# Infini-attention with a GLU: the memory recalls of a segment as sixteen products on the array's quarters, from a dense memory

## The chip, the cores and the metric

The kernel runs on one core of a Trainium2 chip. The metric is device time in microseconds (us), as the median of several runs; smaller is better. A core has TensorE (PE in the profile; its weight loads are PEld), VectorE (DVE), ScalarE (ACT), GpSimd (POOL) and SyncE (SP), which work side by side and wait for one another through semaphores. SP and POOL also issue DMAs; a queue issues in order, so a DMA that waits for its data holds up those behind it. TensorE's results go to PSUM, eight banks of 128 partitions x 512 f32.

## The reference

Two branches read the same normalised input, and both are added to x:

```python
xn = _layernorm(x, axis=-1)
return x + _A_ref(xn, A_wq, A_wk, A_wv, A_wo, A_beta) + _B_ref(xn, B_w_gate, B_w_up, B_w_down)
```

x has 2048 rows of 448. `_B_ref` is a gated FFN, `(sigmoid(xn Wg) * (xn Wu)) Wd`, of inner width 1792. `_A_ref` splits the rows into 4 segments of L = 512 and the columns into 16 heads of 28:

```python
for s in range(N):
    qs, ks, vs = q[:, :, s], k[:, :, s], v[:, :, s]
    logits = jnp.einsum("bhqd,bhkd->bhqk", qs, ks) * scale + mask
    p = _softmax(logits, axis=-1)
    a_dot = jnp.einsum("bhqk,bhkd->bhqd", p, vs)
    pq = phi(qs)
    num = jnp.einsum("bhld,bhde->bhle", pq, M)
    den = jnp.einsum("bhld,bhd->bhl", pq, z)[..., None] + 1e-6
    a_mem = num / den
    o = g * a_mem + (1.0 - g) * a_dot
    outs.append(o)
    pk = phi(ks)
    M = M + jnp.einsum("bhld,bhle->bhde", pk, vs)
    z = z + jnp.einsum("bhld->bhd", pk)
```

Here phi(t) is t + 1 above zero and exp(t) elsewhere; it is an infini-attention with a memory M (28 x 28 per head) and its normaliser z. `a_mem` is called a recall below. Segment 0 has none, since its memory is empty.

## The kernel before

Most products are made of f32 halves: each f32 operand is split into a high and a low part (type fp32r), and `TERMS` lists the 11 products of parts that make one exact product over the 448 columns. A block is a segment of 512 tokens, b = 0 to 3, in four pieces t of 128.

The program has two phases. In the first, the pool `front`, the order of PE, ACT and DVE is the order of the source; SP and POOL are ordered by the scheduler. In the second, PE and SP keep the source's order: three generators are interleaved there, `ffn` (the gated FFN), `attention()` (scores, softmax, and the products with the values, L672) and `project()`. The `ffn` starts in the last block of `front` already, a step for each `next(ffn)`.

In `front`, each block goes through these steps.

- `values(b, t)` (L334): the values of 128 tokens, 11 products into the bank pair `p`; ACT stores them as `vst`, each head in 32 columns: 28 values, then ones. The ones make z a column of the memory.
- `keys_queries(b, c)` (L339), c = 0 to 6: 128 rows of keys and queries, transposed, 448 of each. ACT and DVE split them into `qk`, and SP writes them to `qd` in DRAM (L352). ACT and DVE also make phi of them in `e`; the queries' phi (c from 3) goes to `fd` in DRAM by an SP DMA (L357).
- `key_rows` (L359): TensorE transposes phi of the keys into `kn`, tokens on partitions.
- `update(b, i)` (L369), i = 0 to 3 for a group of four heads: keys by values, four matmuls into a 112 x 128 bank; a mask `heads` keeps the blocks on the diagonal, and the result is added to `mst[n][i]`. A group's memory is thus a block diagonal, 112 rows (4 heads of 28) by 128 columns (4 heads of 32), mostly zeros, in two copies that change places with each block.
- `phi_queries(b, i)` (L381): an SP DMA brings group i's 112 rows of `fd` back to SBUF, from partition 0 on. It shares the five buffers tagged `e`.
- `recall(b, i, phi)` (L386): one f32 matmul, 112 x 128 by 512 tokens, into bank `m` or `pd`. The trace shows an f32 matmul as two passes. DVE then turns it (`ts`, L391: transposes of 32 x 32 blocks), weighs it by the gate and by 1 / z (`weigh`, L127 to L131), and turns it back (`tb`, L393); one POOL DMA writes it to `od` in DRAM (L394), to which attention's part is added later.

Block b has the four recalls of segment b-1, for b = 2 and 3: one after each of values 1, 2 and 3, and one after the first keys. The recalls of segment 3, the last, stand in the last block: after its sixth and seventh `keys_queries` (k = 5 and 6), and then after two steps each (`FILLS`) of the `ffn`. Each recall has a bank, a `ts` (one buffer) and a `tb` (two).

Further names: `ready_down` splits a down weight (`wdn`, ACT and DVE, L85 and L86) that `load_down` brought by SP (`rawd` or `raw`, L185); `begin` holds three such steps that run in the last block. `ready_up` does this for `wgu`. In the FFN, a pair of banks holds the gate and the up product (L240); ACT takes the tanh of the gate into `sg` (L248), DVE multiplies (L249), and ACT and DVE split the result into `hh` (L251, L252). `sg` is one of two buffers of `two_k` (512 f32 per partition). The banks are `p` 2, `s` 2, `m` 1, `gu` 2 and `pd` 1; the gate products take `gu`, the up products `p`, the scores `s` (L597, copied out by ACT, L601).

`G.tensor_copy` in `normalise` lets POOL copy the tail of a normalised piece that `turn` (L95) transposes for the next block.

Of the kernel before, what the change touches and what calls it, by code (L numbers as in the profile page):

```python
# [16 lines left out]
P = 128  # L17
D = 448
# [39 lines left out]
WARM = 10  # L58


@with_exitstack
def kernel(
# [56 lines left out]
    gate = keep.tile([P, NG], F32, name="gate")  # L119
# [148 lines left out]
    with tc.tile_pool(name="front", bufs=2) as sb, tc.manual_schedule(engines=FRONT):  # L268
        heads = sb.tile([P, P], F32, name="heads", bufs=1)
# [5 lines left out]
        mst = [[sb.tile([GW, P], F32, name=f"mst{n}_{i}", bufs=1) for i in range(NG)] for n in range(2)]  # L275
# [63 lines left out]
        def keys_queries(b, c):  # L339

            qk = four_k(F32R, "qk")
            pp = bank("pp", ("p", "gu" if b < NB - 1 else "s")[c % 2])
            for n, (a, w) in enumerate(TERMS):
                T.matmul(pp, wqk[c][:, w, :], xs[b][:, a, :], start=n == 0, stop=n == len(TERMS) - 1)  # L344
            A.activation(qk[:, 0, :], pp, AF.Copy)
            e = None
            if (c < 4 and b < NB - 1) or (c > 2 and b > 0):
                e = sb.tile([P, L], F32, name="e", tag="e", bufs=5)
                A.activation(e, pp, AF.Relu, scale=-1.0)  # L349
                A.activation(e, e, AF.Exp, scale=-1.0)  # L350
            V.tensor_sub(qk[:, 1, :], pp, qk[:, 0, :].bitcast(F32))  # L351
            nc.sync.dma_start(qd[b][c * P:(c + 1) * P], qk.bitcast(F32))  # L352
            if e is not None:
                V.scalar_tensor_tensor(e, pp, 0.0, e, op0=ALU.max, op1=ALU.add)
                if c > 2 and b > 0:
                    lo = max(c * P - D, 0)
                    nc.sync.dma_start(fd[b][lo:(c + 1) * P - D], e[D + lo - c * P:])  # L357
            return e

        def key_rows(c, e):  # L360

            pk = bank("pk", ("m", "pd")[c % 2])
            for t in range(NT):
                T.transpose(pk[:, t * P:(t + 1) * P], e[:, t * P:(t + 1) * P], ident)  # L364
            n = min(P, D - c * P)
            A.activation(kn[:, :, c * P:c * P + n], pk.rearrange("p (t n) -> p t n", t=NT)[:, :, :n], AF.Copy)

        def update(b, i):

            pmm = bank("pmm", ("pd", "m")[i % 2])  # L370
            for t in range(NT):
                T.matmul(pmm[:GW, :P], kn[:, t, i * GW:(i + 1) * GW], vst[:, t, HG * i:HG * (i + 1), :],  # L372
                         start=t == 0, stop=t == NT - 1)
            if b == 0:
                V.tensor_mul(mst[1][i], pmm[:GW, :P], heads[:GW])
            else:
                dm = sb.tile([GW, P], F32, name="dm")
                V.tensor_mul(dm, pmm[:GW, :P], heads[:GW])
                V.tensor_add(mst[(b + 1) % 2][i], mst[b % 2][i], dm)

        def phi_queries(b, i):  # L381
            phi = sb.tile([GW, L], F32, name="phi", tag="e", bufs=5)
            nc.sync.dma_start(phi, fd[b][i * GW:(i + 1) * GW])
            return phi

        def recall(b, i, phi):  # L386
            ts = sb.tile([P, L], F32, name="ts", bufs=1)
            tb = sb.tile([P, L], F32, name="tb", bufs=2)
            n2 = bank("n2", ("m", "pd")[i % 2])
            T.matmul(n2, mst[b % 2][i], phi, start=True, stop=True)  # L390
            V.transpose(ts, n2)  # L391
            weigh(sb, ts, gate[:, i:i + 1], MEM_EPS)
            V.transpose(tb, ts)  # L393
            nc.gpsimd.dma_start(od[b][P * i:P * (i + 1)], tb)  # L394
# [18 lines left out]
        with nc.allow_non_contiguous_dma(reason="a strip's heads"):  # L413
            for j in range(HG):
                nc.sync.dma_start(gate[32 * j:32 * j + 32], beta[j::HG].partition_broadcast(32))
# [50 lines left out]
        for t in range(2):  # L466
# [18 lines left out]
        G.memset(heads, 1.0)  # L485
        h3 = heads.rearrange("p (j c) -> p j c", c=32)
        G.affine_select(h3, h3, pattern=[[-DH, HG], [0, 32]], base=0, channel_multiplier=1,
                        compare_op=ALU.is_ge, fill=0.0)
        G.affine_select(h3, h3, pattern=[[DH, HG], [0, 32]], base=DH - 1, channel_multiplier=-1,
                        compare_op=ALU.is_ge, fill=0.0)  # L490

        ffn = gated()
        for b in range(NB):
            last = b == NB - 1
            phi, xn = {}, {}
            if b > 1:
                phi = {i: phi_queries(b - 1, i) for i in range(NG)}
            st = None
            for t in range(3 if b == 0 else 0, NT):
                values(b, t)  # L500
                if b > 1 and t > 0:
                    recall(b - 1, t - 1, phi[t - 1])
# [15 lines left out]
            for k, c in enumerate((3, 4, 5, 6, 0, 1, 2) if last else range(7)):  # L518
# [3 lines left out]
                if k == 0:  # L522
                    if b > 1:
                        recall(b - 1, NG - 1, phi[NG - 1])
# [4 lines left out]
                    if b == 0:  # L529
# [3 lines left out]
                        V.tensor_scalar(gate_n, gate, -1.0, 1.0, op0=ALU.mult, op1=ALU.add)  # L533
                if last:
                    if k > 0:
                        next(ffn)
                    if 2 <= k < 6:
                        phi[k - 2] = phi_queries(b, k - 2)
                    if k > 4:
                        begin[k - 5]()  # L540
                        recall(b, k - 5, phi[k - 5])
# [14 lines left out]
            if last:  # L556
                for i in range(2):
# [4 lines left out]
                    recall(b, i + 2, phi[i + 2])  # L562
# [256 lines left out]
```

## Time and profile before

| | |
|---|---|
| median of 3 runs | 697.25 us (696.43 to 699.18) |
| span of the profiled execution | 697.6 us |
| TensorE | 690.0 us busy, 99% of the span, 3594 instructions |
| VectorE | 570.2 us, 82% |
| ScalarE | 343.6 us, 49% |
| GpSimd | 148.5 us, 21% |
| DMA packets | 45797, 84.37 MB, mean 121 GB/s |
| DMA issues of recalls: `phi<-fd`, `od<-tb` | 12 each, of 224 and 256 KB |

The profile is of one execution. A timeline row begins with the start in us from the span's start and the time to its last end; "x11" is a run of eleven instructions shown as one row, and its length contains the fill of the array, so that successive rows overlap. In a table of stretches, each engine's busy time and number of instructions follow the bounds and the length (PE, DVE, ACT, POOL, SP), then come the granted TensorE clock, the DMA engines' busy share and GB/s. A row of grouped instructions has the count, the busy sum and the mean of one in ns, then the idle time ahead of them and what ended it. "<-" names what was waited for. The chain of waits follows the end back to what released each step, so its shares say which work sets the time.

### The profile page before, as it was taken

To read this page: it belongs to the slowest core of one execution; us is meant where nothing else is said; L and a number is where in the kernel's file an instruction comes from. 1 tells how busy PE (TensorE), PEld (TensorE's weight loads), DVE (VectorE), ACT (ScalarE), POOL (GpSimd) and SP (SyncE) were. 2 spreads that over 40 slices of the span, in tenths; PEclk is the share of its full clock that TensorE was granted. 3 is DMA by queue.
4 is the path that set the end of the run, shared out by engine and by line. 5 is a ranking of instruction groups with operands and counts; after the bars stand their busy time and mean duration, and the time that the engine had idled before them with its cause. 6 is when DMAs were issued, how large, how long until landed. Compare 5 with 4: busy or idle time off the path is not lost.

```text
span 697.6 us, 10438 instructions
## 1 busy us (share of the span) xinstructions
PE 690.0 (99%) x3594; PEld 567.7 (81%) x3594; DVE 570.2 (82%) x994; ACT 343.6 (49%) x563; POOL 148.5 (21%) x349
## 2 busy tenths in 40 slices
PE   8989999999999999999999999999999999999997
PEld 7878878777878787877878778787787878778897
DVE  6665687658789898988898889998898889889863
ACT  5646646344455455543655446455644555446320
POOL 4400010101222131322222222132221322222000
PEclk9999999999999999999999999999999999999999
DMA  7833545687222423234323343324242432333342
GB/s 265 320 130 149 201 185 211 226 300 224 70 77 65 120 86 85 48 113 108 78 58 96 70 128 66 98 56 114 74 108 66 95 70 60 86 94 88 91 152 105
DMA packets 45797, 84.37 MB, mean 121 GB/s; under 512 B 6321, under 2 KB 20401, under 8 KB 45233
## 3 DMA queue, kind: packets, MB, share of 16 engines
q1 hardware_dynamic: 42736, 76.37, 35.3%
q0 software_dynamic: 3008, 7.34, 5.2%
q8 instruction: 28, 0.46, 0.3%
q14 instruction: 25, 0.20, 0.1%
HBM read 51.05 MB, written 32.64 MB: 120 GB/s over the span
## 4 chain that ended last, share of the span: by engine, by line
PE 94%; DMA 2%; DVE 1%; ACT 1%; SPq 0%; issue 0%; ACTq 0%
PE pgu L240 42%; PE pd L166 20%; PE pp L344 9%; PE st L597 5%; PE pa L672 5%; PE po L756 5%; PE pv L326 4%; PE pmm L372 2%; PE n L390 1%; DMA qd<-qk 1%; DMA acc<-in_x 1%; PE pt L95 1%; PE pk L364 1%; DVE stats L285 0%; ACT L512 0%
## 5 line engine op out<-in xcount | busy, mean ns | idle before, releaser
L240 PE MATMUL pgu<-xs,wgu 128*128 128x512 f32 x1232 | 321.0, 398 | 0.0
L240 PEld LDWEIGHTS pgu<-xs,wgu 128*128 128x128 f32 x1232 | 226.6, 188 | 48.0 <-issue 3.2
L166 PE MATMUL pd<-wdn,hh 128*128 128x448 f32 x672 | 162.4, 368 | 0.0
L612 POOL TENSOR_SCALAR_AFFINE_SELECT w<-w 128x256 f32<-128x256 f32 (+1 forms) x160 | 81.7, 512 | 254.1 <-ACT w L601 215.1
L166 PEld LDWEIGHTS pd<-wdn,hh 128*128 128x128 f32 x672 | 123.2, 188 | 15.1 <-issue 1.0
L652 ACT ACTIVATE w<-w 128x1024 f32<-128x1024 f32 (+1 forms) x96 | 87.1, 915 | 87.6 <-DVE w L651 87.0
L651 DVE TENSOR_TENSOR w<-w,mb 128x1024 f32<-128x1024 f32 (+1 forms) x96 | 99.7, 1049 | 0.2
L601 ACT ACTIVATE w<-st 128x512 f32<-128x512 f32 x128 | 75.0, 588 | 43.6 <-PE st L597 43.5
L614 DVE TRANSPOSE_TENSOR_REDUCE mx<-w 128x32 f32<-128x1024 f32 x64 | 79.1, 1235 | 12.7 <-POOL w L612 12.7
L344 PE MATMUL pp<-xs,wqk 128*128 128x512 f32 x308 | 80.6, 412 | 0.0
L344 PEld LDWEIGHTS pp<-xs,wqk 128*128 128x128 f32 x308 | 58.1, 192 | 14.8 <-issue 2.4
L169 DVE TENSOR_TENSOR acc<-pd,acc 128x448 f32<-128x448 f32 x112 | 67.4, 602 | 2.7 <-PE pd L166 2.5
L597 PE MATMUL st<-qk 84*128 84x128 f32 (+3 forms) x256 | 64.0, 311 | 0.0
L251 ACT ACTIVATE hh<-sg 128x512 fp32r<-128x512 f32 x56 | 35.1, 627 | 44.5 <-DVE sg L249 35.0
L597 PEld LDWEIGHTS st<-qk 84*128 84x128 f32 x256 | 48.4, 189 | 8.6 <-ACT w L601 0.2
L248 ACT ACTIVATE sg<-pgu 128x512 f32<-128x512 f32 x56 | 33.3, 594 | 40.1 <-PE pgu L240 40.1
L641 DVE STREAM_TRANSPOSE mb<-top 128x1024 f32<-128x1024 f32 x32 | 39.8, 1242 | 10.3 <-POOL top L638 10.1
L351 DVE TENSOR_TENSOR qk<-pp,qk 128x512 fp32r<-128x512 f32 x28 | 19.3, 688 | 34.6 <-ACT e L349 27.3
L249 DVE SCALAR_TENSOR_TENSOR sg<-sg,pgu 128x512 f32<-128x512 f32 x56 | 37.4, 668 | 4.8 <-PE pgu L240 4.8
L252 DVE SCALAR_TENSOR_TENSOR hh<-sg,hh 128x512 fp32r<-128x512 f32 x56 | 38.6, 690 | 2.7 <-ACT hh L251 2.5
L326 PE MATMUL pv<-wv,xs 128*128 128x448 f32 x176 | 39.7, 377 | 0.3
L672 PE MATMUL pa<-w,vv 128*32 128x128 f32 (+3 forms) x512 | 38.4, 436 | 0.0
(100 smaller groups left out, 639.2 us busy)
## 6 DMA issues: line engine op xcount, KB each, us to landing
qk<-qd SPq DMA_DIRECT2D x192, 112.0 KB
qd<-qk SPq DMA_DIRECT2D x28, 512.0 KB
raw<-in_w_ffn SPq DMA_DIRECT2D x14, 512.0 KB
vd<-vst SPq DMA_DIRECT2D x4, 1024.0 KB
vv<-vd SPq DMA_DIRECT2D x16, 256.0 KB
od<-w POOLq DMA_DIRECT2D x16, 256.0 KB, 4.0
sums<-od SPq DMA_DIRECT2D x32, 128.0 KB
out<-acc SPq DMA_DIRECT2D x16, 224.0 KB
```

What stands on the lines that cost most here:

```text
L166: T.matmul(pd[:, :D], l, r, start=n == 0, stop=n == len(mms) - 1)
L169: V.tensor_add(acc[b][:, t, :], pd[:, :D], acc[b][:, t, :])
L240: T.matmul(dst, wgu[f][:, w, side * P:(side + 1) * P], xs[b][:, a, :], start=n == 0, stop=n == len(TERMS) - 1)
L326: T.matmul(pv[:, :D], xs[b][:, a, t * P:(t + 1) * P], wv[w], start=n == 0, stop=n == len(TERMS) - 1)
L344: T.matmul(pp, wqk[c][:, w, :], xs[b][:, a, :], start=n == 0, stop=n == len(TERMS) - 1)
L597: T.matmul(st[:, at:at + L - kb * P], self.qk[:KS, 1, h, kb * P:(kb + 1) * P], self.qk[:KS, 0, h, kb * P:], start=True, stop=True)
L601: A.activation(w, st, AF.Copy)
L612: G.affine_select(d, d, pattern=pattern, base=0, channel_multiplier=-1, compare_op=ALU.is_ge, fill=MASK)
L614: V.tensor_reduce(mx[:, 16 * (n - 1):16 * (n + 1)], w3[:, n // 2, :2 * L].rearrange("p (b n) -> p b n", n=32), axis=mybir.AxisListType.X, ...
L651: V.tensor_sub(w, w, m)
L652: A.activation(w, w, AF.Exp, scale=SCALE)
L672: T.matmul(pa[32 * j:32 * j + 32, kb * P:], self.vv[:, kb, 32 * j:32 * j + 32], self.pairs[j // 2].block(j % 2, kb), start=kb == 0, stop=k ...
```

## The change

The memory is kept dense. `update(b, j)` multiplies the values of a group of heads (128 columns, as the stationary operand) by its keys: `by_head` reads the keys in four overlapping runs of 32 columns, 28 apart, so that each head's block is 32 x 32. DVE transposes the 128 x 128 result into `dm`, and after the fourth group copies the diagonal blocks of all groups into one 128 x 128 tile, by four copies or additions. Head 4j + i then has its memory at partitions 32i and columns 32j. The columns of `kn` past the last key are set to zero by POOL; the mask `heads` is gone.

`phi_queries` fills one tile, 128 x 4 x 512, by four SP DMAs: DMA i brings the i-th head of all four groups (28 partitions, four rows of 2 KB for each partition) to partitions 32i.

`recall` is one set of sixteen f32 matmuls, each of 28 rows by 32 columns and 512 tokens at its own position of the array, into four banks: row quarter i into bank i. It stands after values 1 of blocks 2 and 3, and in the last block, for segment 3, after the first FILLS of the `ffn`. `recalled(b, i, n2)` does with bank i what the recall's second half did, with `ts` from the buffers of `two_k`, and with four POOL DMAs of 32 partitions (64 KB) in place of one. It stands where the recalls stood in blocks 2 and 3, and after the two FILLS in the last block, two each. A second gate vector has the heads in the new order, filled by four more small DMAs at the start; the buffers tagged `e` are 4, not 5.

```diff
@@ -56,6 +56,7 @@
 FRONT = {mybir.EngineType.PE, mybir.EngineType.Activation, mybir.EngineType.DVE}
 FILLS = (2, 2)
 WARM = 10
+EB = 4
 
 
 @with_exitstack
@@ -116,7 +117,7 @@
         return ps.tile([P, L], F32, name=name, tag=tag, bufs=banks[tag])
 
 
-    gate = keep.tile([P, NG], F32, name="gate")
+    gate = keep.tile([P, NG + HG], F32, name="gate")
     gate_n = keep.tile([P, NG], F32, name="gate_n")
 
     def weigh(pool, num, g, add):
@@ -266,13 +267,12 @@
 
 
     with tc.tile_pool(name="front", bufs=2) as sb, tc.manual_schedule(engines=FRONT):
-        heads = sb.tile([P, P], F32, name="heads", bufs=1)
         stage = eight_k(F32, "stage").rearrange("p (c a) n -> p c (a n)", c=4)
         vst = eight_k(F32, "vst").rearrange("p (t a) (h c) -> p t (a h) c", t=NT, c=32)
         wv = [late_pair("wv") for _ in range(4)]
         wv = [wv[c // 2][:, c % 2, :] for c in range(8)]
         wqk = [sb.tile([P, 8, P], F32R, name=f"wqk{c}", bufs=1) for c in range(7)]
-        mst = [[sb.tile([GW, P], F32, name=f"mst{n}_{i}", bufs=1) for i in range(NG)] for n in range(2)]
+        mst = [sb.tile([P, P], F32, name=f"mst{n}", bufs=1) for n in range(2)]
         one = sb.tile([P, 1], F32, name="one", bufs=1)
         kn = eight_k(F32, "kn").rearrange("p (t a) n -> p t (a n)", t=NT)
 
@@ -345,7 +345,7 @@
             A.activation(qk[:, 0, :], pp, AF.Copy)
             e = None
             if (c < 4 and b < NB - 1) or (c > 2 and b > 0):
-                e = sb.tile([P, L], F32, name="e", tag="e", bufs=5)
+                e = sb.tile([P, L], F32, name="e", tag="e", bufs=EB)
                 A.activation(e, pp, AF.Relu, scale=-1.0)
                 A.activation(e, e, AF.Exp, scale=-1.0)
             V.tensor_sub(qk[:, 1, :], pp, qk[:, 0, :].bitcast(F32))
@@ -357,6 +357,10 @@
                     nc.sync.dma_start(fd[b][lo:(c + 1) * P - D], e[D + lo - c * P:])
             return e
 
+        def by_head(a):
+
+            return bass.AP(a.tensor, a.offset, [list(a.ap[0]), [DH, HG], [1, 32]])
+
         def key_rows(c, e):
 
             pk = bank("pk", ("m", "pd")[c % 2])
@@ -365,33 +369,52 @@
             n = min(P, D - c * P)
             A.activation(kn[:, :, c * P:c * P + n], pk.rearrange("p (t n) -> p t n", t=NT)[:, :, :n], AF.Copy)
 
-        def update(b, i):
-
-            pmm = bank("pmm", ("pd", "m")[i % 2])
+        turned = {}
+
+        def update(b, j):
+
+            if j == 0:
+                turned[b] = two_k("dm").rearrange("p (j n) -> p j n", n=P)
+            dm = turned[b]
+            pmm = bank("pmm", ("pd", "m")[j % 2])
             for t in range(NT):
-                T.matmul(pmm[:GW, :P], kn[:, t, i * GW:(i + 1) * GW], vst[:, t, HG * i:HG * (i + 1), :],
-                         start=t == 0, stop=t == NT - 1)
-            if b == 0:
-                V.tensor_mul(mst[1][i], pmm[:GW, :P], heads[:GW])
-            else:
-                dm = sb.tile([GW, P], F32, name="dm")
-                V.tensor_mul(dm, pmm[:GW, :P], heads[:GW])
-                V.tensor_add(mst[(b + 1) % 2][i], mst[b % 2][i], dm)
-
-        def phi_queries(b, i):
-            phi = sb.tile([GW, L], F32, name="phi", tag="e", bufs=5)
-            nc.sync.dma_start(phi, fd[b][i * GW:(i + 1) * GW])
-            return phi
-
-        def recall(b, i, phi):
-            ts = sb.tile([P, L], F32, name="ts", bufs=1)
+                keys = by_head(kn[:, t, GW * j:GW * j + HG * 32])
+                T.matmul(pmm[:, :P], vst[:, t, HG * j:HG * (j + 1), :], keys, start=t == 0, stop=t == NT - 1)
+            V.transpose(dm[:, j, :], pmm[:, :P])
+            if j == HG - 1:
+                for i in range(NG):
+                    rows = slice(32 * i, 32 * i + 32)
+                    after, before = (mst[(b + n) % 2][rows, :].rearrange("p (j c) -> p j c", c=32) for n in (1, 0))
+                    if b == 0:
+                        V.tensor_copy(after, dm[rows, :, rows])
+                    else:
+                        V.tensor_add(after, before, dm[rows, :, rows])
+
+        def phi_queries(b, phi):
+            for i in range(HG):
+                nc.sync.dma_start(phi[32 * i:32 * i + DH],
+                                  fd[b].rearrange("(j i d) n -> i d j n", i=HG, d=DH)[i])
+
+        def recall(b, phi, tags):
+
+            n2 = [bank("n2", tag) for tag in tags]
+            for i in range(HG):
+                rows = slice(32 * i, 32 * i + DH)
+                for j in range(NG):
+                    cols = slice(32 * j, 32 * j + 32)
+                    T.matmul(n2[i][cols, :], mst[b % 2][rows, cols], phi[rows, j, :], start=True, stop=True,
+                             tile_position=(32 * i, 32 * j))
+            return n2
+
+        def recalled(b, i, n2):
+            ts = two_k("ts")
             tb = sb.tile([P, L], F32, name="tb", bufs=2)
-            n2 = bank("n2", ("m", "pd")[i % 2])
-            T.matmul(n2, mst[b % 2][i], phi, start=True, stop=True)
-            V.transpose(ts, n2)
-            weigh(sb, ts, gate[:, i:i + 1], MEM_EPS)
+            V.transpose(ts, n2[i])
+            weigh(sb, ts, gate[:, NG + i:NG + i + 1], MEM_EPS)
             V.transpose(tb, ts)
-            nc.gpsimd.dma_start(od[b][P * i:P * (i + 1)], tb)
+            for j in range(NG):
+                h = HG * j + i
+                nc.gpsimd.dma_start(od[b][32 * h:32 * h + 32], tb[32 * j:32 * j + 32])
 
         raw = [four_k(F32, "wv_raw") for _ in range(2)]
         raw = [r.rearrange("p a n -> p (a n)")[:, :2 * D] for r in raw]
@@ -412,7 +435,9 @@
         nc.sync.dma_start(raw_qk[6], w_qk[6])
         with nc.allow_non_contiguous_dma(reason="a strip's heads"):
             for j in range(HG):
-                nc.sync.dma_start(gate[32 * j:32 * j + 32], beta[j::HG].partition_broadcast(32))
+                nc.sync.dma_start(gate[32 * j:32 * j + 32, :NG], beta[j::HG].partition_broadcast(32))
+            for j in range(NG):
+                nc.sync.dma_start(gate[32 * j:32 * j + 32, NG:], beta[HG * j:HG * j + HG].partition_broadcast(32))
         G.memset(vst[:, :, :, DH:], 1.0)
         A.activation(gate_n, vst[:, 0, :NG, DH], AF.Sqrt)
 
@@ -482,24 +507,22 @@
         turn_low(3)
         split_qk(1)
         split_qk(2)
-        G.memset(heads, 1.0)
-        h3 = heads.rearrange("p (j c) -> p j c", c=32)
-        G.affine_select(h3, h3, pattern=[[-DH, HG], [0, 32]], base=0, channel_multiplier=1,
-                        compare_op=ALU.is_ge, fill=0.0)
-        G.affine_select(h3, h3, pattern=[[DH, HG], [0, 32]], base=DH - 1, channel_multiplier=-1,
-                        compare_op=ALU.is_ge, fill=0.0)
+        G.memset(kn[:, :, D:], 0.0)
 
         ffn = gated()
         for b in range(NB):
             last = b == NB - 1
-            phi, xn = {}, {}
+            xn = {}
             if b > 1:
-                phi = {i: phi_queries(b - 1, i) for i in range(NG)}
+                phi = sb.tile([P, NG, L], F32, name="phi", bufs=1)
+                phi_queries(b - 1, phi)
             st = None
             for t in range(3 if b == 0 else 0, NT):
                 values(b, t)
+                if b > 1 and t == 1:
+                    n2 = recall(b - 1, phi, ("gu", "gu", "m", "pd"))
                 if b > 1 and t > 0:
-                    recall(b - 1, t - 1, phi[t - 1])
+                    recalled(b - 1, t - 1, n2)
                 if b == 0:
                     split_qk(t)
                 if last:
@@ -521,7 +544,7 @@
                     split_qk(c + 4)
                 if k == 0:
                     if b > 1:
-                        recall(b - 1, NG - 1, phi[NG - 1])
+                        recalled(b - 1, NG - 1, n2)
                     if b == 0:
                         st = rstd(*st)
                     if b < 2:
@@ -530,15 +553,15 @@
                         A.activation(gate, gate, AF.Exp, scale=-1.0)
                         V.tensor_scalar_add(gate, gate, 1.0)
                         V.reciprocal(gate, gate)
-                        V.tensor_scalar(gate_n, gate, -1.0, 1.0, op0=ALU.mult, op1=ALU.add)
+                        V.tensor_scalar(gate_n, gate[:, :NG], -1.0, 1.0, op0=ALU.mult, op1=ALU.add)
                 if last:
                     if k > 0:
                         next(ffn)
-                    if 2 <= k < 6:
-                        phi[k - 2] = phi_queries(b, k - 2)
+                    if k == 3:
+                        phi = sb.tile([P, NG, L], F32, name="phi", bufs=1)
+                        phi_queries(b, phi)
                     if k > 4:
                         begin[k - 5]()
-                        recall(b, k - 5, phi[k - 5])
                     continue
                 if 2 <= k < 6:
                     key_rows(k - 2, e[k - 2])
@@ -559,7 +582,9 @@
                         next(ffn)
                     if i == 0:
                         begin[2]()
-                    recall(b, i + 2, phi[i + 2])
+                        n2 = recall(b, phi, ("s", "s", "m", "pd"))
+                    recalled(b, 2 * i, n2)
+                    recalled(b, 2 * i + 1, n2)
 
 
 
```

## The prediction

> **What bounds the kernel now.** First the page's busy shares and the chain of work that ended last.
>
> ```profile
> PE 690.0 (99%) x3594; PEld 567.7 (81%) x3594; DVE 570.2 (82%) x994; ACT 343.6 (49%) x563; POOL 148.5 (21%) x349
> ...
> PE pgu L240 42%; PE pd L166 20%; PE pp L344 9%; PE st L597 5%; PE pa L672 5%; PE po L756 5%; PE pv L326 4%; PE pmm L372 2%; PE n L390 1%; DMA qd<-qk 1%; DMA acc<-in_x 1%; PE pt L95 1%; PE pk L364 1%; DVE stats L285 0%; ACT L512 0%
> ```
>
> TensorE sets the time, and its order is fixed: a microsecond that it waits is lost, one taken from it is won. The recalls (L390) are 1% of the chain. So I read the TensorE timeline where they stand: segment 1's (three rows), segment 2's first, segment 3's last.
>
> ```profile
> 82.42 4.66 PE L326 MATMUL pv<-wv,xs 128*128 128x448 f32 x22
> 86.92 1.02 PE L390 MATMUL n<-phi,mst 112*128 112x512 f32 x2
> 87.38 2.78 PE L326 MATMUL pv<-wv,xs 128*128 128x448 f32 x11
> 90.00 1.02 PE L390 MATMUL n<-phi,mst 112*128 112x512 f32 x2
> ...
> 124.14 1.02 PE L390 MATMUL n<-phi,mst 112*128 112x512 f32 x2
> ...
> 155.26 0.86 PE L240 MATMUL pgu<-xs,wgu 128*128 128x512 f32 x3
> 155.96 1.02 PE L390 MATMUL n<-phi,mst 112*128 112x512 f32 x2
> ...
> 161.63 7.33 PE L240 MATMUL pgu<-xs,wgu 128*128 128x512 f32 x29
> 168.79 0.40 PE L597 MATMUL st<-qk 84*128 84x512 f32 x1
> ...
> 172.47 0.40 PE L597 MATMUL st<-qk 84*128 84x512 f32 x1
> ```
>
> The shown durations overlap, so costs come from starts. From 86.92 to 90.00 are 3.08 us; 11 value matmuls take half of 4.66 less overlap, 2.21. A recall therefore costs 0.87, two passes of 0.43, and a segment's four 3.47. None of them waits here.
>
> **Part 1, the sixteen products.** Thirty-two passes of 28 rows by 32 columns replace eight. The trace has no product by row quarters; the nearest is the attention product L672, four column quarters with full rows.
>
> ```profile
> 207.72 0.16 PEld L672 LDWEIGHTS pa<-w,vv 128*32 128x32 f32 x8 [0.36 <-POOL w L612]
> 208.18 0.13 PEld L672 LDWEIGHTS pa<-w,vv 128*32 128x32 f32 x4 [0.30 <-issue]
> ```
>
> Weight loads come four at a time, 0.46 us apart: four column quarters share one pass time. Whether row quarters share it too no row shows. Bounds for a segment: 0.87 if all sixteen go together, 4 x 0.87 = 3.47 if only columns do; about 0.3 beside for filling and emptying (also an estimate, from 1.02 against 0.87 twice). I take 1.17: a gain of 2.3 per segment.
>
> The Trainium skill, "TensorEngine Tiling (Array Packing)", Key Properties, lets tiles on different rows and columns run at the same time; by that it is the lower bound, as I took, and the L672 row agrees for columns.
>
> **Part 2, waiting for phi, segments 1 and 2.** Before, copy i needed only its 112 rows, and recalls stood after the second, third and fourth values and the next keys, so that each came 3 us after the one before. Now copy i takes 28 rows from each of the four groups: all four copies need the last feature write (c=6), and all sixteen products stand after the second values.
>
> ```profile
> 83.46 0.32 SPq L357 DMA_DIRECT2D fd<-e  x1
> 86.35 0.79 SPq L383 DMA_DIRECT2D phi<-fd  x2
> ...
> 120.75 0.42 SPq L357 DMA_DIRECT2D fd<-e  x1
> ...
> 124.67 0.79 SPq L383 DMA_DIRECT2D phi<-fd  x2
> ...
> 87.00:87.50 0.50, 0.50 (x4) 0.26 (x2) 0.43 (x3) 0.00 (x0) 0.00 (x0) 1.00 0.40 61
> ...
> 87.25:89.00 1.75, 1.75 (x9) 1.33 (x8) 1.29 (x5) 0.64 (x2) 0.00 (x0) 1.00 0.84 260
> ...
> 206.29 2.47 SPq L580 DMA_DIRECT2D qk<-qd  x6
> 207.25:210.75 3.50, 3.50 (x38) 1.70 (x37) 3.20 (x7) 0.94 (x2) 0.89 (x2) 1.00 0.80 195
> ```
>
> (SP queue; then tables of stretches, last two columns DMA share and GB/s.) The last write is issued at 83.46; the first copies that need it start at 86.35, 2.89 later, and their data rises within about 0.9. So in the changed kernel all four copies start at 86.35, and TensorE is at the recalls at 86.92: it is there before the data. How fast 224 KB land: 112-partition copies ran at 260 GB/s, the 28-partition copies of qk at 195. The new ones have 28 partitions, so I take 195: 1.18 us each (0.86 by 260). First landing near 86.35 + 0.9 + 1.2 + about 0.4 until the semaphore (an estimate) = 88.8, the fourth 3.5 later, 92.3. Rows 0 to 2 run meanwhile; the last row's passes take 0.87 + 0.15, so that values go on at 93.4. Before, TensorE would have had the two values and four recalls behind it, had they stood together, at 86.92 + 3.47 = 90.4. Loss **+3.0**; bounds +1.3 (260 GB/s for all and no time until the semaphore: 86.35 + 0.9 + 3.4 + 1.0 = 91.7) and +4 (1.4 until the semaphore).
>
> Segment 2: TensorE at 124.14, old products done at 127.6; the write issued at 120.75 has landed after the same 2.89 at 123.6, or by the row only at 124.67. The same 7.0 from there to the next values gives +3.0 and +4.1; between them **+3.5**, bounds +1.3 and +4.8. Queued behind the wait on TensorE are the third and fourth values and the keys, so everything that follows.
>
> **Part 3, segment 3.** All sixteen products now stand after the first FFN fill; nothing waits for data there, as the copies are issued four keys earlier. That saves 2.3. But the drain moves to the FFN's start. The order of the changed streams: VectorE must do three recalls before the first multiply of the second gated pair; the recalls' `ts` now shares the two `sg` buffers, so the second and third tanh (L248) wait until `ts` of recalls 2 and 3 are turned into `tb`. And two loads (rawd, raw) now stand on SP behind the write of the last key block.
>
> ```profile
> 87.95:90.68 2.73, 2.29 (x4) 1.00 0.37 127
> ...
> L394 POOL DMA_DIRECT2D od<-tb x12 | 6.7, 559 | 88.2 <-DVE tb L393 85.7 <-DVE tm L304 2.5
> ...
> 152.99 0.35 SPq L185 DMA_DIRECT2D rawd<-in_w_ffn  x1
> 156.81 0.33 SPq L352 DMA_DIRECT2D qd<-qk  x1
> ...
> 158.41 0.56 ACT L85 ACTIVATE wdn<-rawd 128x448 fp32r<-128x448 f32 x1
> 158.68 0.62 DVE L86 TENSOR_TENSOR wdn<-raw,wdn 128x448 fp32r<-128x448 f32 x1
> 160.05 1.22 DVE L86 TENSOR_TENSOR wgu<-raw,wgu 128x1024 fp32r<-128x1024 f32 x1
> 160.44 0.60 ACT L248 ACTIVATE sg<-pgu 128x512 f32<-128x512 f32 x1 [0.52 <-PE pgu L240]
> 163.95 0.67 DVE L249 SCALAR_TENSOR_TENSOR sg<-sg,pgu 128x512 f32<-128x512 f32 x1
> 170.32 0.58 ACT L601 ACTIVATE w<-st 128x512 f32<-128x512 f32 x1
> ```
>
> The first row is one whole recall on VectorE (transpose, weighing, transpose): 2.73. Counted as if nothing before had shifted, the three pgu matmuls start at s = 155.26 - 0.87 = 154.4, since the recall ahead of them (one of two among the last keys) is gone. rawd is issued right behind the write, 156.81 - 0.87 + 0.4 = 156.3; it lands about 3 later (as the 2.89), 159.3; ACT and VectorE split it until 160.5; three recalls and the wgu split, 3 x 2.7 + 1.2 = 9.3, end at 169.8; tanh 0.6: 170.4. TensorE needs that tanh's bank for the fourth pair's gate. A pgu matmul takes 0.23 (29 from 161.63, behind 0.4 of a recall's second pass, to 168.79). Eleven stand ahead of the products, 2.6; products 1.2; then 36 matmuls, 8.4, and a score product, 0.24: it is there at 154.4 + 12.4 = 166.8: stall 3.65. Then VectorE has the fourth `ts`, sg, weighing, hh and `tb`, about 3.6 in all, until 173.8; tanh, sg, hh and the score copy follow with 0.6 each, so the third score product starts at about 176.4, before at 172.47: **+4.0**. Bounds: -2.3 if VectorE keeps up, +5. Were rawd not late, 1.4 less of the stall and +2.5.
>
> **Nothing for the rest.** The update has its four matmuls per group as before and the same number of VectorE operations: ±0.2 by the count. POOL issues 36 more DMAs of 0.56, 20 us of an engine that is 21% busy; its copies for block 3's transposes can stand behind one recall's four, 2.2 us, for which the wait of Part 2 leaves time; with that cover gone, up to +1. Fewer `e` buffers and four small gate loads at the start: covered by loads that SP waits for anyway, ±0.2.
>
> **Sum.** 697.6 + 3.0 + 3.5 + 4.0 = 708.1 against the profiled span; the median of the runs is 0.35 below that span: **708**.
>
> **The rivals.** *The pack without a wait* (faster): the sixteen products start when TensorE gets there. Place: TensorE at 86.92 and 124.14. Point: the fourth copy must land within about 0.9 after that, by 87.8 and 125.0; then 3 x -2.3 = -6.9, 690.4. For it: products do shrink from 3.47 to 1.17. Against: with a write landing at 86.35 the four copies, 0.9 MB, would need over 600 GB/s. *The waits, but no drain problem*: VectorE catches up in segment 3, since its 82% leave room; 697.25 + 3.0 + 3.5 - 2.3 = 701.5. For it: had the loads held nothing up, 9.3 us of work from 157.2, when the first products are out, would end at 166.5, just in time. Against: the loads do stand behind a write, and the shared buffers stay. *Copies land at the 260 rate and complete at once*: Part 2 falls to +1.3 twice: 703.9 with Part 3 at +4.0, 697.6 with Part 3 at -2.3. *The clock*: each wait cools TensorE.
>
> ```profile
> L431 PE MATMUL warm<-ident 128*128 128x128 f32 x20 | 4.6, 430 | 1.5 <-POOL ident masks.py:199 1.5
> ...
> L364 PE MATMUL pk<-ident,e 128*128 128x128 f32 x48 | 7.2, 272 | 0.0
> ```
>
> At the start 20 matmuls took 4.6 us; the same shape later 7.2 x 20 / 48 = 3.0. If each of three waits costs that 1.6 again, 708 + 4.8 = 712.8. The waits are 1 to 4 us long and broken by products of other rows, so perhaps one or none. The Trainium skill, "TensorE: Matmul & The Clock Gate", Part 1, says that some 3.4 us without work halve the clock; by it the stretches here stay mostly just under. *The change does not do what it says*: row quarters follow one another. Then the copies' pitch of 1.18 hides 0.87 per row and the total stays; only if all sixteen go one by one, 13.9 per segment, is it about +35: 733.
>
> **How the numbers follow.** My forecast 60% (its own range 703 to 711), waits without drain problem 17%, fast copies 8%, clock 7%, one by one 3%, pack without a wait 5%. A difference of 0.5%, 3.5 us, is about what a measurement of this kernel can tell from none: 693.8 to 700.7. Faster: the pack without a wait, 0.05. Same: fast copies without drain problem and the lower ends of the waits alone, 0.09. Slower: the rest, 0.86. The range leaves out the pack and one by one, and cuts the clock's tail and the fastest copies: 700 to 712.
>
> **What would show it.** Right: TensorE's idle before the recalls at about 87 and 124, ended by DMA phi, 3 to 5 us in all at each, products of a row under 1.1 us; idle in the FFN's first pairs ended by ACT's tanh, itself waiting on VectorE `tb`; rawd issued after the last qd. Wrong: products starting without a wait; L248 not waiting on L393; rows of the product 3 us apart on a busy TensorE; a granted clock below 1 behind the waits.

## The result, and the profile after

| | median | lowest to highest | ratio to before (95%) |
|---|---|---|---|
| before | 697.16 us | 696.43 to 699.18 | |
| changed | 717.44 us | 715.02 to 719.75 | 1.0283 (1.026 to 1.0307) |

The change costs 20.3 us; 708 with a range of 700 to 712 had been predicted. The direction and the places were right, the size was half.

First the device time and the span. The changed kernel's profiled execution took 716.85 us and its span is 715.1; a second profile of the kernel before (run e4 below) took 697.08 with a span of 695.4. So the time is the span and about 1.7 us, and the first profile of before, with its span of 697.6, came from an execution some 2 us above the median. The stages below are therefore counted against e4's profile. These are rows of its TensorE timeline: the first values of block 2, the first transposes behind segment 1's recalls, the first FFN product behind segment 2's, and the first down product behind segment 3's.

```profile
80.21 1.05 PE L326 MATMUL pv<-wv,xs 128*128 128x448 f32 x4
...
97.71 0.60 PE L95 MATMUL pt<-ident,xn 128*128 128x128 f32 x4
...
134.92 1.10 PE L240 MATMUL pgu<-xs,wgu 128*128 128x512 f32 x4
...
169.66 0.76 PE L166 MATMUL pd<-wdn,hh 128*128 128x448 f32 x3
```

The same places in the changed kernel, with all that lies between them at the three recalls:

```profile
78.54 4.65 PE L326 MATMUL pv<-wv,xs 128*128 128x448 f32 x22
...
85.66 5.43 PE L405 MATMUL n<-phi,mst 28*32 28x512 f32 x32 [2.47 <-DMA phi<-fd]
91.02 7.23 PE L326 MATMUL pv<-wv,xs 128*128 128x448 f32 x22
98.08 5.29 PE L344 MATMUL pp<-xs,wqk 128*128 128x512 f32 x22
103.21 0.60 PE L96 MATMUL pt<-ident,xn 128*128 128x128 f32 x4
...
130.02 5.50 PE L405 MATMUL n<-phi,mst 28*32 28x512 f32 x32 [2.36 <-DMA phi<-fd]
135.45 7.19 PE L326 MATMUL pv<-wv,xs 128*128 128x448 f32 x22
142.49 5.29 PE L344 MATMUL pp<-xs,wqk 128*128 128x512 f32 x22
147.62 1.09 PE L241 MATMUL pgu<-xs,wgu 128*128 128x512 f32 x4
...
164.88 2.73 PE L241 MATMUL pgu<-xs,wgu 128*128 128x512 f32 x11
167.54 1.14 PE L405 MATMUL n<-phi,mst 28*32 28x512 f32 x32
168.62 8.66 PE L241 MATMUL pgu<-xs,wgu 128*128 128x512 f32 x36
178.60 0.47 PE L622 MATMUL st<-qk 84*128 84x512 f32 x1 [1.32 <-DMA qk<-qd]
183.93 3.78 PE L241 MATMUL pgu<-xs,wgu 128*128 128x512 f32 x8 [4.86 <-ACT sg L249]
...
189.04 0.76 PE L167 MATMUL pd<-wdn,hh 128*128 128x448 f32 x3
```

| up to | before (e4) | changed | difference | of this stage |
|---|---|---|---|---|
| first values of block 2 | 80.21 | 78.54 | -1.7 | start: -1.7 |
| transposes in block 2 | 97.71 | 103.21 | +5.5 | segment 1: +7.2 |
| first FFN product | 134.92 | 147.62 | +12.7 | segment 2: +7.2 |
| first down product | 169.66 | 189.04 | +19.4 | segment 3: +6.7 |
| end of the span | 695.4 | 715.1 | +19.7 | the rest: +0.3 |

In segments 1 and 2 the reader sees two losses. One is the wait of about 2.4 us in brackets and the products that follow the landings, 5.4 us in place of 1.14. The other stands behind them: the 22 value matmuls take 7.06 us to the next row's start, where 11 took 2.2 before, so 2.6 us too much. A table of stretches of the changed kernel (busy time of each engine; the last three columns are the granted clock, the DMA share and GB/s) says why:

```profile
84.00:86.00 2.00, 0.34 (x4) 0.15 (x8) 0.35 (x2) 0.64 (x2) 0.00 (x0) 1.00 0.95 206
86.00:88.00 2.00, 2.00 (x16) 0.20 (x8) 0.89 (x2) 0.00 (x0) 0.00 (x0) 0.57 0.93 187
88.00:90.00 2.00, 2.00 (x16) 0.42 (x16) 1.90 (x4) 0.00 (x0) 0.00 (x0) 0.50 0.03 5
...
94.00:96.00 2.00, 2.00 (x6) 1.78 (x6) 1.75 (x7) 0.47 (x1) 1.40 (x4) 0.50 0.46 98
96.00:98.00 2.00, 2.00 (x10) 1.83 (x9) 0.56 (x2) 1.56 (x3) 1.62 (x5) 0.87 0.59 131
```

TensorE's clock is halved from about 86.3 to 96.5, ten microseconds for a wait of 2.5. In segment 3 it is halved again, from the end of the wait of 4.86 on: eight FFN products take 3.57 us from start to start of what follows, in place of 1.86.

What VectorE, ScalarE and SP do ahead of that wait:

```profile
166.82 0.43 SPq L186 DMA_DIRECT2D rawd<-in_w_ffn  x1
...
171.12 0.58 ACT L86 ACTIVATE wdn<-rawd 128x448 fp32r<-128x448 f32 x1 [2.99 <-DMA rawd<-in_w_ffn]
173.87 1.06 ACT L86 ACTIVATE wgu<-raw 128x1024 fp32r<-128x1024 f32 x1 [2.17 <-DMA raw<-in_w_ffn]
183.28 0.60 ACT L249 ACTIVATE sg<-pgu 128x512 f32<-128x512 f32 x1 [8.34 <-DVE tb L414]
...
182.47 0.71 DVE L414 STREAM_TRANSPOSE tb<-ts 128x512 f32<-128x512 f32 x1 [1.28 <-DMA od<-tb]
```

The load issued at 166.82 reaches ScalarE at 171.1; the second tanh starts after ScalarE has stood idle for 8.3 us, and what ends this is the third drain's `tb`; and that `tb` itself waits 1.3 us until the writes of the first one have left the buffer.

### The profile page after: what moved, and what is told of

It is laid out like the page before. It is cut to its first block, busy times and chain, and to the rows that moved or that the text cites. A ratio compares the mean times of both kernels' runs of the same rounds, so it can differ in the third digit from the quotient of the medians.

```text
span 715.1 us, 10635 instructions
## 1 busy us (share of the span) xinstructions
PE 697.2 (97%) x3666; PEld 567.9 (79%) x3666; DVE 572.5 (80%) x998; ACT 343.8 (48%) x563; POOL 164.6 (23%) x383
## 4 chain that ended last, share of the span: by engine, by line
PE 92%; DMA 3%; DVE 2%; ACT 1%; issue 0%; POOL 0%; SPq 0%; DVEq 0%; ACTq 0%
PE pgu L241 39%; PE pd L167 19%; PE pp L344 10%; PE st L622 5%; PE pa L697 5%; PE po L781 5%; PE pv L326 4%; PE n L405 2%; PE pmm L382 1%; DMA raw<-in_w_ffn 1%; DMA phi<-fd 1%; PE pt L96 1%; DMA fd<-e 1%; PE pk L368 1%; DMA od<-tb 1%
## 5 line engine op out<-in xcount | busy, mean ns | idle before, releaser
L344 PE MATMUL pp<-xs,wqk 128*128 128x512 f32 x308 | 76.7, 398 | 0.0
L417 POOL DMA_DIRECT2D od<-tb x48 | 23.9, 505 | 95.5 <-DVE tb L414 94.6
L326 PE MATMUL pv<-wv,xs 128*128 128x448 f32 x176 | 43.0, 403 | 0.3 <-POOL wv L446 0.2
L326 PEld LDWEIGHTS pv<-wv,xs 128*128 128x128 f32 x176 | 36.4, 212 | 7.5 <-issue 3.3
```

The source lines that it names most:

```text
L326: T.matmul(pv[:, :D], xs[b][:, a, t * P:(t + 1) * P], wv[w], start=n == 0, stop=n == len(TERMS) - 1)
```

## The experiments

Each compares with the kernel before on the same chip; "717.4" in what was expected is the changed kernel.

| run | what | median us | ratio to before (95%) |
|---|---|---|---|
| e1 | filler of 18 and 4 in the wait | 719.55 | 1.0319 (1.0302 to 1.0336) |
| e2 | products after values 3 | 707.79 | 1.0153 (1.0138 to 1.0169) |
| e3 | own buffers for the turned recalls | 714.95 | 1.026 (1.0238 to 1.0282) |
| e4 | before, again | 697.08 | one run |
| e5 | filler of 10 and 1 | 718.66 | 1.0286 (1.0248 to 1.0324) |
| e6 | values 2, phi in eight copies | 705.83 | 1.0102 (1.006 to 1.0144) |
| e7 | segment 3's products and drains earlier | 711.13 | 1.0175 (1.0138 to 1.0211) |
| e8 | e6 and e7 together, load first | 697.69 | 1.0001 (0.9983 to 1.002) |
| e9 | before, with four more small loads | 696.86 | 0.9986 (0.9973 to 1.0) |
| e10 | e8, one drain moved | 694.18 | 0.9951 (0.9934 to 0.9967) |
| e11 | load first, alone | 713.1 | 1.0217 (1.0191 to 1.0242) |

**e1 and e5: is the halved clock due to the wait?** Both put small matmuls into it.

```diff
+                if spare is not None:
+                    for _ in range(18 if i == 0 else 4):    # e5: 10 if i == 0 else 1
+                        T.matmul(spare[:, :P], ident, ident, start=True, stop=True)
```

> Twenty-two small f32 matmuls of the identity (128 x 128, into a spare bank) more per segment, 18 ahead of the first row of products and 4 ahead of each later row of segments 1 and 2, fill TensorE's wait for phi; nothing else changes. Theory (the wait also halves the granted clock, and the halved clock costs as much as the wait): the clock stays at 1.00 in that stage, the 22 value matmuls behind the products take 4.5 us again in place of 7.0, the stage loses 3 to 4 us per segment, time 717.4 - 7 = 710.5, within 708.5 to 712.5. Rival (the wait for phi alone is the loss, and the values behind it are slow for another reason, traffic or PSUM): the values stay at 7 us, time 717 to 719.

> The filler of the first try cut to the wait: 10 small matmuls of the identity (20 passes, 2.2 us) ahead of the first row of products and one ahead of each later row, in segments 1 and 2. Theory (clock): granted clock 1.00 throughout, the products' passes 0.45 in place of 0.86, the 22 values behind them 4.5 us in place of 7.0; 3.4 us less per segment, time 717.4 - 6.9 = 710.5, within 709 to 712.5. Rival (the clock is beside the point, the data alone set the pace): time 716 to 718.5.

Both missed their times and came out just above even the rivals' ranges (719 and 718.5), so by the time alone the theory would be wrong. e1's filler was too long: each of these matmuls is two passes (36 instructions for 18), so that it took 4.18 us for a wait of 2.5, and the values start at 94.53 in place of 91.02. What the filler cost was thus as much as the clock gave back. But its clock stayed at 1.00, and the values behind it took 4.5 us:

```profile
83.19 4.18 PE L405 MATMUL spare<-ident 128*128 128x128 f32 x36
87.30 1.06 PE L408 MATMUL n<-phi,mst 28*32 28x512 f32 x8
88.30 1.16 PE L405 MATMUL spare<-ident 128*128 128x128 f32 x8
...
94.53 4.68 PE L326 MATMUL pv<-wv,xs 128*128 128x448 f32 x22
```

In e5 the filler fits, TensorE stands idle for less than 0.1 us before the first row, and the clock falls all the same:

```profile
83.05 2.39 PE L405 MATMUL spare<-ident 128*128 128x128 f32 x20
85.52 1.06 PE L408 MATMUL n<-phi,mst 28*32 28x512 f32 x8
86.51 0.49 PE L405 MATMUL spare<-ident 128*128 128x128 f32 x2
86.93 1.06 PE L408 MATMUL n<-phi,mst 28*32 28x512 f32 x8
...
88.34 1.40 PE L408 MATMUL n<-phi,mst 28*32 28x512 f32 x8
...
90.39 1.93 PE L408 MATMUL n<-phi,mst 28*32 28x512 f32 x8
92.25 6.30 PE L326 MATMUL pv<-wv,xs 128*128 128x448 f32 x22
```

```profile
86.00:88.00 2.00, 2.00 (x19) 0.53 (x11) 1.25 (x4) 0.00 (x0) 0.00 (x0) 1.00 0.87 176
88.00:90.00 2.00, 2.00 (x11) 0.70 (x12) 1.93 (x4) 0.00 (x0) 0.35 (x1) 0.73 0.03 8
```

A row of products takes 1.06 at first, 1.40 from 88.34, and 1.93 at 90.39; the granted clock falls to 0.73 in the stretch from 88 to 90 with TensorE busy throughout. It is the same in every execution: the mean clock of the span was 0.978 to 0.984 in the four of the changed kernel, 0.982 to 0.985 in e5, and 0.992 to 0.995 in e1. So idle time alone is not what counts here. For some 3 us TensorE had worked almost only on one row quarter at a time, 28 of 128 rows; with as many passes of dense filler as of products (e1) the clock stayed. The reading that fits both is that a row quarter counts as too little work; what the chip counts no run shows directly. My theory, that the wait halves the clock, falls in that form: in segments 1 and 2 the wait and the rows that come one by one can do it together, and the rows alone suffice. Whether the wait would do it with all sixteen in one go behind it, no run shows.

**e2: the products later.**

```diff
-                if b > 1 and t == 1:
+                if b > 1 and t == 3:
```

(with the drains after values 3 and behind the first three keys).

> The sixteen products of segments 1 and 2 stand after values 3 in place of values 1, and the four drains after them one by one; segment 3 is left as it is. Theory (products placed ahead of their data, and the clock lost by that, are all of the loss in segments 1 and 2): TensorE gets there about 4.4 us later, waits under 1 us in all, the clock stays at 1.00; each of the two segments goes from +7.1 to about -1, time 717.4 - 16 = 701.4, within 699 to 704. Rival (the products themselves, 28 rows by 32 columns, are dear, or the four copies slow their neighbours): less than half of that, time above 709.

The two segments did what the theory says: from the first values to the transposes in block 2 they take 95.32 - 78.78 = 16.5 us, 17.5 before, 24.7 in the changed kernel. The time came out 3.8 above the range. Most of that is my edit, which pushed the drains into the keys: key transposes waited 1.38 and 1.65 us for `ts` on a bank that was not yet drained. The rest is in segment 3, where the copies were issued only 4.8 us ahead of the products (7.1 in the changed kernel), and which from the first FFN product to the first down product took 1.8 us longer. It gave a second case of the clock, in the same timeline:

```profile
156.50 1.94 PE L405 MATMUL n<-phi,mst 28*32 28x512 f32 x16
158.81 2.75 PE L405 MATMUL n<-phi,mst 28*32 28x512 f32 x16 [0.38 <-DMA phi<-fd]
161.50 11.15 PE L241 MATMUL pgu<-xs,wgu 128*128 128x512 f32 x36
```

Idle for 0.38 us only, but 5 us on products of one or two row quarters; the 36 FFN products behind them take 11.15 in place of 8.66.

**e3, e7 and e11: segment 3.** e3 gives the turned recalls other buffers; e11 moves the load; e7 moves the products ahead of the fills, with e3's buffers.

```diff
-            ts = two_k("ts")
+            ts = sb.tile([P, L], F32, name="ts", tag="e", bufs=EB)
```

```diff
-        begin.extend([lambda: ready_down(0), lambda: (ready_down(1), load_down(2)), lambda: ready_down(2)])
+        begin.extend([lambda: (ready_down(0), load_down(2)), lambda: ready_down(1), lambda: ready_down(2)])
```

```diff
                     if k > 4:
                         begin[k - 5]()
+                    if k == 6:
+                        n2 = recall(b, phi, ("m", "pd", "s", "s"))
+                        recalled(b, 0, n2)
+                        recalled(b, 1, n2)
...
-                        n2 = recall(b, phi, ("s", "s", "m", "pd"))
-                    recalled(b, 2 * i, n2)
-                    recalled(b, 2 * i + 1, n2)
+                    recalled(b, i + 2, n2)
```

> The turned recalls (ts) take a buffer of the tag e, as no tanh of the FFN does, in place of the two that they share with sg. Theory (the shared buffers tie the second tanh of the FFN to the third drain): that tanh no longer waits for tb, TensorE's 4.9 us of idle before the fourth pair shrinks to under 2 and the clock stays up there; time 717.4 - 4 = 713.4, within 711.5 to 715. Rival (VectorE is late anyway, because the late down weight holds its queue): the tanh runs earlier but TensorE then waits for the multiply instead, time 716 to 718.

> The changed kernel with one move: the load of the third down weight is put ahead of the write of the last keys in SP's queue, as the kernel of before had it. Theory (the late load starts the drains late, as the prediction's third part has it): the split of that weight and the first drain come 1.4 to 2.5 us earlier on VectorE, and TensorE's idle before the fourth pair shrinks by as much; time 717.4 - 2 = 715.4, within 714 to 716.3. Rival (the drains are held by their own buffers, so an earlier start only lengthens the wait for them): 716.8 to 718.

> Segment 3 alone: the sixteen products stand behind the last keys, ahead of the FFN's fills, with two drains there and one after each fill, and the turned recalls do not share the tanh's buffers; segments 1 and 2 as in the changed kernel. Theory (the late start of the drains and the shared buffers are the loss there): TensorE's 1.3 + 4.9 us of idle go, the clock stays; segment 3 goes from +6.7 to about -1, time 717.4 - 7.7 = 709.7, within 708 to 711.5. Rival (VectorE has no room for four drains in a row there): 713 or more.

e3 and e7 fell into their ranges (e3 by 0.05, with single executions from 712.5 to 717.1), e11 gained more than its own (4.3 us, of which 0.9 stand ahead of its first FFN product, at 146.75, and can't be its doing). With e3 the tanh no longer waits, but half of the gain is lost again three rows on: TensorE then stands before the first down product, whose bank holds the fourth recall.

```profile
183.04 1.46 PE L167 MATMUL pd<-wdn,hh 128*128 128x448 f32 x3 [4.24 <-DVE ts L412]
```

With e11 the idle before the fourth pair falls from 1.32 + 4.86 to 3.51. So the load and the shared buffers each carry a part, and neither all of it. Earlier products and drains together with the buffers (e7) bring most: 717.44 - 711.13 = 6.3 us of this segment's 6.7, without reaching the saving of 2.3 beside. What the earlier place alone would bring, no run shows.

**e6, e8 and e10: segments 1 and 2, and all together.**

```diff
-            for i in range(HG):
-                nc.sync.dma_start(phi[32 * i:32 * i + DH],
-                                  fd[b].rearrange("(j i d) n -> i d j n", i=HG, d=DH)[i])
+            for j in (0, 2):
+                for i in range(HG):
+                    nc.sync.dma_start(phi[32 * i:32 * i + DH, j:j + 2],
+                                      fd[b][j * GW:(j + 2) * GW].rearrange("(j i d) n -> i d j n", i=HG, d=DH)[i])
...
-                if b > 1 and t == 1:
+                if b > 1 and t == 2:
```

> Segments 1 and 2 alone: the products stand after values 2 in place of values 1, and phi comes in eight copies of 112 KB, four of which (groups 0 and 1) do not need the last feature write. Theory (place and late data are the loss there): TensorE waits under 1 us, the clock stays at 1.00, each of the two segments goes from +7.1 to about -1.3; time 717.4 - 16.8 = 700.6, up to 704 if the drains, pushed into the keys, make a bank late. Rival (smaller copies are slower, or their issue on SP takes the time): above 706.

> Both of these together, and the load of the down weight issued ahead of the last key write. Theory: 717.4 - 16.8 - 7.7 = 692.9, within 691 to 696, so faster than the kernel of before by 2 to 6 us: the products do save 2.3 us a segment when nothing waits for them. Rival (the saving is always given back in a wait elsewhere): 697 or more.

> As the run with both remedies, but the fourth drain of segment 1 stands behind the normalising of the next block's third piece in VectorE's order, not ahead of it. In the run before, that piece was late, TensorE stood 1.7 us in two pieces at 102 and 104 us, and a key product behind it took 4.36 us in place of 2.8. Theory: both go, 3.8 us less, time 697.7 - 3.8 = 693.9, within 692.5 to 695.5: faster than before. Rival (VectorE is simply full there and the wait moves to the next piece): 696 to 698.

e6 and e8 came out 1.8 and 1.7 us above their ranges, 5.2 and 4.8 above the theory's own figures: e6 just short of its rival's 706, e8 where its rival has it. In both, TensorE is no longer idle before the products, and the values behind them run at full clock. But the sixteen take 2.2 to 2.6 us there in place of 1.14, as weight loads still wait 0.2 to 0.9 us for the last copies. And in both a drain in front of the next block's normalising makes that late (these rows are e6's):

```profile
85.24 2.29 PE L406 MATMUL n<-phi,mst 28*32 28x512 f32 x32
87.47 2.48 PE L326 MATMUL pv<-wv,xs 128*128 128x448 f32 x11
...
102.82 0.52 PE L96 MATMUL pt<-ident,xn 128*128 128x128 f32 x3 [0.87 <-DVE xn L311]
104.21 0.33 PE L96 MATMUL pt<-ident,xn 128*128 128x128 f32 x1 [0.87 <-POOL xn L317]
```

In e8 the key product behind these two waits took 4.36 us, at a halved clock:

```profile
104.15 4.36 PE L344 MATMUL pp<-xs,wqk 128*128 128x512 f32 x11
```

In e6 the same product behind the same two waits took 2.81 at full clock, so a fall of the clock behind such waits is not certain. The larger part of e6's miss is in segment 3, which its edit does not touch: the two waits there grew from 1.32 + 4.86 to 2.28 + 7.08 us.

e10 puts that drain behind the normalising; both waits are gone from its timeline, and it gains 3.5 us on e8. At 694.18 us it is the one version clearly faster than before, by 0.49% (0.33 to 0.66). Not all of that is the products' doing. Its profile is 3.5 us ahead of e4's (one execution each), and 1.7 of these stand before the first recall, as in the changed kernel. The three stages bring 1.1, 0.9 and 1.4 more, and 1.3 are lost again right behind the first down product, where TensorE waits 1.01 for ScalarE. So the rival of e8, that the saving is always given back, falls, but of the 2.3 us a segment that the products can save some 0.7 are left.

**e4 and e9: the start.** The changed kernel is 1.7 us ahead before its first recall, which no part of the prediction has.

> The kernel of before once more, unchanged, for a second profile. If the wait of 2.1 us for kn at 36.7 us and the slow stage behind it belong to the kernel of before in every execution, it shows them again and the span is 696 to 698; if they belong to that one execution, the wait is gone or shorter and the span is 693.5 to 695.5.

> The kernel of before with four more small loads of beta at its start, into a tile that nothing reads; recalls as they were. With them SP's queue has the FFN's first weights behind the first key writes, as in the changed kernel, and not ahead of them. Theory (that order, not the recalls, is why the changed kernel is 1.7 us ahead before its first recall): no wait for kn at 34 us, the first values of block 1 start at 44.7 as in the changed kernel in place of 46.5, time 697.0 - 1.7 = 695.3, within 694.3 to 696.3. Rival (the update or the fewer buffers made it): 696.5 to 698.

```diff
+            gx = sb.tile([P, NG], F32, name="gx", bufs=1)
+            for j in range(NG):
+                nc.sync.dma_start(gx[32 * j:32 * j + 32], beta[HG * j:HG * j + HG].partition_broadcast(32))
```

e4 shows a shorter wait for `kn` and no slow stage behind it, with a span of 695.4; that is the second case, so a part of both belongs to the first execution alone. Before, TensorE waits for `kn`, and `kn` for ScalarE, which waits for a buffer of `qk` until its write to DRAM is done; in e4 TensorE's wait was 1.48 us (2.14 and a slow stage in the first profile), in the changed kernel nothing. SP's queue shows the difference: e4 first, then the changed kernel.

```profile
15.93 3.41 SPq L178 DMA_DIRECT2D raw<-in_w_ffn  x2
20.68 0.33 SPq L332 DMA_DIRECT2D vd<-vst  x1
21.06 0.43 SPq L185 DMA_DIRECT2D rawd<-in_w_ffn  x1
25.08 21.14 SPq L352 DMA_DIRECT2D qd<-qk  x7
```

```profile
24.88 0.32 SPq L352 DMA_DIRECT2D qd<-qk  x1
25.25 0.45 SPq L179 DMA_DIRECT2D raw<-in_w_ffn  x1
29.57 1.94 SPq L352 DMA_DIRECT2D qd<-qk  x2
31.57 0.42 SPq L186 DMA_DIRECT2D rawd<-in_w_ffn  x1
```

Before, three weight loads stand ahead of the first key write; now two of the three come later. e9's four loads moved only one of them behind the key writes (the second raw is still issued at 21.00), its wait fell to 0.87, and the time by 0.6, with an interval that ends at 1.0: the time of the rival. That the order is the whole of the 1.7 us is thus likely, not shown.

## Why the prediction was half right

- *The products*: right, where all data are there: sixteen together take 1.14 us in segment 3; 1.17 was predicted. So row quarters do work at once, the lower bound of part 1.
- *The wait for phi, segments 1 and 2*: right as a mechanism. The copies start at 82.27, 2.74 us after the issue of the last write (2.89 predicted), and land at 206 and 187 GB/s (195). From the end of the second values to the third ones 7.8 us pass; with the four old recalls it would be 3.47. Predicted were 6.5 in segment 1, so this term is 1.3 too small: the last row of products takes 0.9 more at half clock (1.86 in place of 0.99, as in e5's rows), and the rest is a later landing: the last row could start 6.9 us after the copies, 5.95 was estimated.
- *The step that failed*: the cost of the wait was taken as the time that TensorE stands and no more. The clock was named, as a rival of 7% with 1.6 us for each wait, "broken by products of other rows, so perhaps one or none". It came in all three. In segments 1 and 2 it costs 2.6 us on the values and 0.9 on the products, in segment 3 about 2.3: from the wait's end to the first down product 5.11 us pass, where 11 products of 0.23 and two score products would take 2.8. Together that is 2 x 3.5 + 2.3 = 9.3 us; the three stages cost 21.1 us where 10.5 were forecast. The products of single rows, which I took for a help, are in part the cause (e5). The last of the prediction's own signs of being wrong, a clock below 1 behind the waits, is what came. The rival's 712.8 is the closest of the forecasts, with 4.8 us for the clock, about half of the real price.
- *The Trainium skill's rule*, "TensorE: Matmul & The Clock Gate", Part 1, was read there as a matter of time without work alone. That the 1.48 us of idle in e4 left the clock full agrees with that reading. But less than 0.1 us without work went with a halved clock (e5), and so did 2.5 us of idle with rows of products behind it. There the measurement decides: a stretch of some 3 us with little of the array at work was enough.
- *Segment 3*: right as a mechanism, too small. TensorE is to be at the fourth pair at s + 12.4 = 177.3 and goes on at 183.93: 6.65 us, predicted 3.65. The load was issued where it was predicted (s + 1.94), but reached ScalarE 1.3 us later than the estimate; the other load, for `wgu`, held the first drain 0.8 us; and the third drain waited 1.3 us for its buffer's writes, which the prediction doesn't have. The second stall of 2.6 us did not come, most likely because the first one had given VectorE the time (in e3, where the first is gone, one of 4.24 does come). That these two errors, 3.0 too little and 2.6 too much, nearly cancel is luck; what is left of the 2.7 us by which this stage was too small is the halved clock.
- *What was costed at nothing*: the update holds (sixteen matmuls 1.95 us, 1.91 before). The four small loads may not be nothing: alone (e9) they moved one of two weight loads behind the key writes and brought 0.6 us, with an interval that reaches zero, so the gain of 1.7 us at the start stays in part open. POOL's copies had the time that the prediction gave them, in the wait of segment 1; in e6 and e8, where that wait is gone, they and the normalising are late.

## What to carry to other kernels

A product made cheaper by packing is worth its saving only where its operands have landed and its drain has room: here 2.3 us a segment were bought, and late data, a late load, shared buffers and the halved clock made of it a loss of 7 each. A wait on a saturated TensorE is to be priced with the slow stretch that can follow it, which in segments 1 and 2 cost 3.5 us for a wait of 2.4; so place such a product one step later, and split its loads by what each needs. When drains are moved, look at which in-order queue they now stand in front of.

## What the runs showed of the hardware that was not expected

TensorE's granted clock fell to half with TensorE busy throughout: products of 28 rows by 32 columns, one row quarter at a time, for 3 to 4 us (e5, and e2 with 0.38 us idle). It came back after 2.7 to 5.5 us of dense work: the 22 values behind them took 7.06 us in the changed kernel, 6.14 in e5 and 4.5 at full clock. The same sixteen products in one go (1.14 us) left it at 1.00.
